# Gate logits turned by four transposes and summed on VectorE, and expert 0's first product taken in two halves of 256 tokens

## The chip, the cores and the metric

One Trainium2 chip, of which the kernel uses one core. The metric is device time in microseconds (us) of one execution, the median of the runs shown; less is better. A core has TensorE (PE in the rows, its weight loads PEld), VectorE (DVE), ScalarE (ACT), GpSimd (POOL), and SyncE (SP), which issues most of the transfers. Each engine takes its own instructions in the order in which the program gives them; engines wait for each other by semaphores.

## The reference

Three stages follow each other. A delta-rule attention (4 batches, 8 heads, 768 steps, head size 48) gives 3072 tokens of 384 features; a mixture of 8 experts with soft gates takes them; a last layer with x·cos(x) between two products ends it.

```python
for t in range(S):                                   # attention
    y[:, :, t] = einsum('bhd,bhde->bhe', q[:, :, t], state)
    v_old = einsum('bhde,bhd->bhe', state, k_n[:, :, t])
    state = state + beta_t * outer(k_n[:, :, t], v[:, :, t] - v_old)
...
logits = x @ w_gate                                  # 3072 x 8
P = exp(logits - logits.max())
for _ in range(8):                                   # balance rows and columns
    P /= P.sum(1, keepdims=True) + 1e-09
    P /= P.sum(0, keepdims=True) + 1e-09
    P *= N / E
for e in range(E):
    h = maximum(x @ w1[e], 0.0)
    out += P[:, e:e + 1] * (h @ w2[e])
...
h = x @ w_in
return (h * cos(h)) @ w_out
```

## The kernel before, in words

**Units and blocks.** The 768 steps are cut into 12 units of 64 steps; a unit of all heads and batches gives 256 tokens. Two units make a block of 512 tokens, and `xb[m]` holds block m twice, as a high part (written by ScalarE, L577) and a low part (what the high part left over, written by VectorE, L578). Products in the experts are taken as high·high, high·low and low·high, so 384 features in three slices of 128 give nine matmuls of 512 tokens.

**Expert 0 beside the attention.** While the attention runs, TensorE also does expert 0. `moe0_h` takes a *first product* (nine matmuls, `h_mms`, L138) for 128 hidden features of one block into the bank `hb`; ScalarE and VectorE apply the relu and split it in two parts (`relu_split`, L156 and L157). `moe0_y` takes the *second product* (nine matmuls, `yT_mms`, L150) into the three banks `yb[0]` to `yb[2]`. The half steps alternate: first product s+1, then second product s. All first products of this stage use the one bank `hb`, so each waits until VectorE's L157 has read the one before.

**The order** is written out by hand. `SEQ` has a string of letters for each unit, and `tick` runs them in turn on all engines. The string that matters begins `m W G E K r g m N m e O m m`, and belongs to unit 2, the first that works on block 0. `m` is a half step, `G` the gate logits of a block (`pe_gate`, six matmuls into `yb[0]`, copied to SBUF as `ltm`, 16 rows by 512 tokens: the first eight rows and the last eight have to be added), `E` turns queries, `K` multiplies the state with the keys (its difference D is VectorE's L513), `e` takes the query-key products (`pe_GQ`, L312, masked by VectorE's L367), `X` turns a unit's output into `xb` by six transposes (L572).

**The turning of the logits**, `g` (`pe_gate2`), multiplies four slices of 128 tokens of `ltm` by `two`, a 16x8 matrix of two stacked identities, which turns and adds at once (L597), into the first 32 columns of `yb[0]`. ScalarE copies them to `logits` (L600). It happens once for each block, six times: in the strings of units 2, 4, 6, 8, 10 and 11.

**The inverse.** Two units at a time, GpSimd solves small triangular systems in 60 steps, one after the other (L387 and L391), each depending on the last. `r` runs what is left of the steps and then gives VectorE a transpose of the result (`inv_dm`, L451), which waits for GpSimd.

**After the attention** eight rounds of row and column sums balance P: `sk_exp` and `sk_cols`, small matmuls (L622, L635) and VectorE steps, between products of expert 0. The exponential (L624) needs another ScalarE table than what went before, so a table load stands ahead of it. Most of the run, from about 450 us on, is the other experts and the last layer.

Of the kernel before, what the change touches and what calls it, by code (L numbers as in the profile page):

```python
# [8 lines left out]
F32 = mybir.dt.float32  # L9
F32R = mybir.dt.float32r  # L10
ACTF = mybir.ActivationFunctionType
ALU = mybir.AluOpType
# [10 lines left out]
I32 = mybir.dt.int32  # L23
BF16 = mybir.dt.bfloat16

SEQ = ("U0 a0 y1 o2 S0 x1 b0 P0 K1 o3 k1 v U1 X0 P1 S1 X1 x2",
# [12 lines left out]
def kernel(  # L39
# [13 lines left out]
    nc = tc.nc  # L53
    B, H, S, D = q.shape
    NT, DM = out.shape
    E, _, F = w1.shape
# [4 lines left out]
    KD = DM // 128  # L61
# [5 lines left out]
    const = ctx.enter_context(tc.tile_pool(name="const", bufs=1))  # L67
# [15 lines left out]
    hb, yb, pa = ps8[:, 0], [ps8[:, 1 + i] for i in range(KD)], [ps8[:, 4 + i] for i in range(4)]  # L83

    ident = const.tile([128, 128], F32, name="ident")
    wg_sb = const.tile([128, KD, E], F32, name="wg_sb")
    wg = const.tile([128, KD, 2, E], F32R, name="wg")
    logits = const.tile([128, NQ, E], F32, name="logits")
# [5 lines left out]
    Xsys = inv1[:, 0:1024].rearrange("p (t i) -> p t i", i=CB)  # L94
    Nst = inv2[:, 0:1024].rearrange("p (s t) -> p s t", t=CB)
    ltm = inv2[0:2 * E, 1024:1536]
    two = const.tile([2 * E, E], F32, name="two")
    ones = const.tile([128, 128], F32, name="ones")
    small = const.tile([128, 4, 32], F32, name="small")

# [27 lines left out]
        nc.scalar.activation(out=t[:, 0], in_=st, func=ACTF.Copy)  # L128
        eng.tensor_tensor(out=t[:, 1], in0=st, in1=t[:, 0].bitcast(F32), op=ALU.subtract)

    def h_mms(ps, n, f, x, c0, nn):

        w = w1_t[n]
        fs = slice((f % 2) * 128, (f % 2) * 128 + 128)
        i = 0
        for kk in range(KD):
            for a, b in ((0, 0), (0, 1), (1, 0)):
                nc.tensor.matmul(  # L138
                    out=ps[:, :nn], lhsT=w[:, a, kk, fs], rhs=x[:, b, kk, c0:c0 + nn],
                    start=(i == 0), stop=(i == 3 * KD - 1),  # L140
                )
                i += 1

    def yT_mms(banks, n, f, h, first, last):

# [43 lines left out]
    kr, qr, V, KT, QT, Pp, Go, D_t, U_t, Y_t, xb = {}, {}, {}, {}, {}, {}, {}, {}, {}, {}, {}  # L189
# [404 lines left out]

    def pe_gate2(m):
        for i in range(4):
            nc.tensor.matmul(  # L597
                out=yb[0][:, i * E:(i + 1) * E], lhsT=ltm[:, i * 128:(i + 1) * 128], rhs=two, start=True, stop=True,
            )
        nc.scalar.activation(  # L600
            out=logits[:, 4 * m:4 * m + 4, :], in_=yb[0][:, 0:4 * E].rearrange("p (i e) -> p i e", i=4), func=ACTF.Copy
        )


    sk = []
# [59 lines left out]
    def moe0_h(s):  # L665
        m, f = divmod(s, FT)

        if s >= NS0 - 4:
            bank, h = (pa[2], pa[1], pa[0], hb)[s % 4], htile()
        else:  # L670
            bank = pa[0] if scr and s % 2 else hb
            h = hp.tile([128, 2, 512], F32R, tag="h", name="h")
        h_mms(bank, f // 2, f, xb[m], 0, 512)
        relu_split(h, bank, 512)
        h0_t[s] = h

# [17 lines left out]
    with tc.manual_schedule():  # L694
# [36 lines left out]
        for r in range(4):  # L731
            m = m16[r * CB:(r + 1) * CB]
            nc.gpsimd.affine_select(
                out=m, in_=m, pattern=[[1, CB]], compare_op=ALU.is_gt, fill=0.0, base=0, channel_multiplier=-1
# [9 lines left out]
        for b in range(2):  # L744
            m = mask[b * C:(b + 1) * C]
            nc.gpsimd.affine_select(
                out=m, in_=m, pattern=[[1, C]], compare_op=ALU.is_gt, fill=0.0, base=0, channel_multiplier=-1
            )
        nc.gpsimd.memset(St[0], 0.0)
        nc.gpsimd.tensor_tensor(out=two, in0=ident[0:2 * E, 0:E], in1=ident[0:2 * E, E:2 * E], op=ALU.add)  # L750
        nc.gpsimd.memset(ones, 1.0)

        inv_q = []
# [167 lines left out]
        for s in range(NS0 - 1):  # L921
            t = 2 * ((s + 1) // FT) + 2
# [5 lines left out]
        def half():  # L928
            if mq and mq[0][0] <= done[0]:
                _, c, s = mq.pop(0)  # L930
                (moe0_h if c == "h" else moe0_y)(s)
# [9 lines left out]
        def tick(u, seq):  # L941
            early = u < 2
            for x, c in enumerate(seq.split()):
# [4 lines left out]
                    u, c = int(c[1]), c[0]  # L948
                if c == "m":
                    half()  # L950
                elif c == "K":
                    pe_KS(u)
                elif c == "k":
# [970 lines left out]
```

## Time and profile before

| | |
|---|---|
| median of 3 runs | 2100.38 us (2097.69 to 2106.63) |
| the profiled execution | 2102.24 us, of which 2100.5 us is the span from first to last instruction |
| busy TensorE | 2056.9 us, 98% of the span |
| busy VectorE, ScalarE, GpSimd | 1467.1, 859.2, 905.2 us |
| chain of work that ended last | TensorE 91%, DMA 3%, VectorE 2%, GpSimd 2% |
| mean granted TensorE clock | 0.988 of 2.4 GHz |

How to read it: the chain that ended last runs over TensorE nearly throughout, so a microsecond of TensorE work or of TensorE idleness is a microsecond of the run, unless something else sets the pace at that place. TensorE's idle time is 2100.5 - 2056.9 = 43.6 us. The slices of the page show where it lies: in the first 100 us TensorE is busy in seven to nine tenths, later in nine tenths or more of every slice.

### The profile page before, as it was taken

The page shows a single profiled execution, that of the slowest core. Times are in us where ns is not written, and L with a number is a line of the kernel's source. Part 1 is how long each engine was busy: PE and PEld are TensorE (multiplying, and loading weights), DVE is VectorE, ACT ScalarE, POOL GpSimd, SP SyncE. Part 2 cuts the span into 40 slices and gives each one's busy share as a digit, 9 for nine tenths or more (in the row PEclk, how much of TensorE's full clock was granted, in tenths as well). Part 3 has the DMA queues.
Part 4 walks back from the last instruction along what each step waited for, and adds up shares of the span by engine and source line. Part 5 has one row for each costly group of instructions (what it writes and reads, how often), then busy time and mean ns, then how long its engine had stood idle before and what let it go on. Part 6 is the DMA issues. An engine that isn't in the chain of part 4 may idle for free.

```text
span 2100.5 us, 39722 instructions
## 1 busy us (share of the span) xinstructions
PE 2056.9 (98%) x16147; PEld 1732.4 (82%) x16147; DVE 1467.1 (70%) x2247; ACT 859.2 (41%) x1436; POOL 905.2 (43%) x1013
## 2 busy tenths in 40 slices
PE   7899999999999999999999999999999999999999
PEld 6788787778888888888878888888888889999998
DVE  6665546677777777778767778778778666666665
ACT  3343333334444344343333333333333346666664
POOL 4676660136556565454344333333333343333232
PEclk6899999999999999999999999999999999999999
DMA  5442335765455445453684444435353551011000
GB/s 97 109 108 49 85 111 182 264 258 189 151 198 179 165 171 202 138 193 133 242 322 133 163 165 151 150 109 196 139 180 134 177 223 31 1 31 31 16 16 15
DMA packets 212470, 294.39 MB, mean 140 GB/s; under 512 B 86160, under 2 KB 159344, under 8 KB 212288
## 3 DMA queue, kind: packets, MB, share of 16 engines
q1 hardware_dynamic: 209456, 285.08, 40.7%
q0 software_dynamic: 1664, 6.49, 0.9%
q8 instruction: 126, 2.06, 0.4%
q10 hardware_dynamic: 1168, 0.30, 0.1%
q14 instruction: 56, 0.46, 0.1%
HBM read 188.95 MB, written 113.87 MB: 144 GB/s over the span
## 4 chain that ended last, share of the span: by engine, by line
PE 91%; DMA 3%; DVE 2%; POOL 2%; issue 1%; ACT 1%; SPq 0%; POOLq 0%; DVEq 0%; ACTq 0%
PE ps L150 36%; PE ps L1462 26%; PE ps L1752 9%; PE ps L1710 9%; PE ps L138 4%; PE ps L312 1%; PE ps L280 1%; POOL w1t L391 1%; POOL w1t L387 1%; DMA T<-xsc 1%; DMA tp<-in_moe_w_out_dram 1%; DMA wss<-w1t 1%; PE ps L497 1%; PE ps L474 1%; PE ps L462 1%
## 5 line engine op out<-in xcount | busy, mean ns | idle before, releaser
L150 PE MATMUL ps<-mh,w2t 128*128 128x512 f32 x3060 | 749.5, 390 | 1.2 <-DVE cth L1498 1.2
L150 PEld LDWEIGHTS ps<-mh,w2t 128*128 128x128 f32 x3060 | 573.4, 188 | 123.4 <-DVE cth L1498 5.0
L1462 PE MATMUL ps<-T,w1t 128*128 128x512 f32 x2520 | 627.6, 390 | 3.8 <-DVE ps L1470 2.1
L1499 POOL TENSOR_TENSOR accp<-accp,cth 128x512 f32<-128x512 f32 x246 | 320.1, 1330 | 568.3 <-DVE cth L1498 568.2
L1462 PEld LDWEIGHTS ps<-T,w1t 128*128 128x128 f32 x2520 | 472.1, 188 | 104.1 <-DVE ps L1470 3.4
L156 ACT ACTIVATE mh<-ps 128x512 fp32r<-128x512 f32 x340 | 203.4, 599 | 623.9 <-PE ps L1462 237.3
L157 DVE SCALAR_TENSOR_TENSOR mh<-ps,mh 128x512 fp32r<-128x512 f32 x340 | 228.8, 688 | 176.5 <-ACT mh L156 174.8
L1467 ACT ACTIVATE scr<-ps 128x512 f32<-128x512 f32 x224 | 134.4, 600 | 171.0 <-PE ps L1462 164.2
L1719 POOL TENSOR_SCALAR tp<-tp 128x512 f32<-128x512 f32 x92 | 91.1, 990 | 204.6 <-ACT tp L1718 204.6
L1498 DVE TENSOR_TENSOR cth<-ps,scr 128x512 f32<-128x512 f32 x246 | 154.3, 683 | 15.3 <-PE ps L150 14.2
L1733 DVE TENSOR_TENSOR tp<-tp,ps 128x512 f32<-128x512 f32 x96 | 66.1, 688 | 133.5 <-ACT tp L1732 133.5
L1470 DVE TENSOR_TENSOR ps<-scr,ps 128x512 f32<-128x512 f32 x168 | 116.5, 694 | 56.8 <-PE ps L1462 55.4
L138 PE MATMUL ps<-xb,w1t 128*128 128x512 f32 x432 | 114.0, 409 | 5.9 <-DVE h L157 4.5
L138 PEld LDWEIGHTS ps<-xb,w1t 128*128 128x128 f32 x432 | 79.4, 192 | 24.6 <-DVE h L157 4.6
L150 PE MATMUL ps<-h,w2t 128*128 128x512 f32 x396 | 98.5, 393 | 0.0
L1470 DVE TENSOR_TENSOR scr<-ps,scr 128x512 f32<-128x512 f32 x112 | 77.1, 688 | 29.6 <-PE ps L1462 28.7
L1303 DVE TENSOR_TENSOR w1t<-wraw,w1t 128x512 fp32r<-128x512 f32 (+2 forms) x81 | 82.4, 1029 | 9.9 <-ACT w1t L1300 9.5
L391 POOL TENSOR_TENSOR w1t<-w1t 128x30 f32<-128x30 f32 (+9 forms) x150 | 81.5, 543 | 11.8
L150 PEld LDWEIGHTS ps<-h,w2t 128*128 128x128 f32 x396 | 73.3, 188 | 15.3
L1710 PE MATMUL ps<-xx,cw 128*128 128x512 f32 x360 | 84.0, 390 | 0.0
L1718 ACT ACTIVATE tp<-ps 128x512 f32<-128x512 f32 x96 | 56.1, 585 | 63.4 <-PE ps L1710 63.4
L387 POOL TENSOR_TENSOR w1t<-Nsys,w1t 128x30 f32<-128x30 f32 (+9 forms) x150 | 77.0, 514 | 11.4
(286 smaller groups left out, 2769.9 us busy)
## 6 DMA issues: line engine op xcount, KB each, us to landing
wss<-w1t SPq DMA_DIRECT2D x56, 768.0 KB
w1t<-wss SPq DMA_DIRECT2D x56, 768.0 KB
w2t<-w2c SPq DMA_DIRECT2D x56, 384.0 KB
T<-tsc SPq DMA_DIRECT2D x22, 512.0 KB
scr<-pts SPq DMA_DIRECT2D x44, 256.0 KB
w2c<-in_moe_w_dram SPq DMA_DIRECT2D x28, 384.0 KB
wss<-w1t SPq DMA_DIRECT2D x28, 384.0 KB
w1t<-wss SPq DMA_DIRECT2D x28, 384.0 KB
```

Source lines behind the costliest of these rows:

```text
L138: nc.tensor.matmul(out=ps[:, :nn], lhsT=w[:, a, kk, fs], rhs=x[:, b, kk, c0:c0 + nn], start=(i == 0), stop=(i == 3 * KD - 1),)
L150: nc.tensor.matmul(out=banks[kd], lhsT=w[:, a, f % 2, kd * 128:(kd + 1) * 128], rhs=h[:, b, :], start=(first and b == 0 and a == 0), stop= ...
L156: nc.scalar.activation(out=h[:, 0, :nn], in_=ps[:, :nn], func=ACTF.Relu)
L157: nc.vector.scalar_tensor_tensor(out=h[:, 1, :nn], in0=ps[:, :nn], scalar=0.0, in1=h[:, 0, :nn].bitcast(F32), op0=ALU.max, op1=ALU.subtract,)
L391: eng.tensor_tensor(out=xsys[:, j + 1:, 0:j], in0=xsys[:, j + 1:, 0:j], in1=a, op=ALU.add)
L1462: nc.tensor.matmul(out=bank, lhsT=s_of(n, nm, a), rhs=T[:, b, :], start=start and q == 0, stop=q == 2, skip_group_check=True)
L1467: nc.scalar.activation(out=out, in_=in_, func=ACTF.Copy, scale=scale)
L1470: nc.vector.tensor_tensor(out=out, in0=a, in1=b, op=op)
L1498: nc.vector.tensor_tensor(out=c, in0=yb[kd], in1=pslot[t], op=ALU.mult)
L1499: nc.gpsimd.tensor_tensor(out=a[:, kd, :], in0=a[:, kd, :], in1=c, op=ALU.add)
L1710: nc.tensor.matmul(out=hb2(i), lhsT=net_w1(f, a, kk), rhs=x2[b](c, kk), start=(j == 0), stop=(j == 3 * KD - 1))
L1752: nc.tensor.matmul(out=ybk[t][:, :DM], lhsT=h[:, a, ts], rhs=net_w2(f, c), start=(f == 0 and j == 0), stop=(f == FT2 - 1 and j == 2),)
```

## The change

Three things are altered. The turning of the logits uses four transposes of 16 rows instead of four matmuls with `two`, which leaves 16 columns for each token; ScalarE copies the last eight of them to `logits`, and a new VectorE instruction adds the first eight from the bank. The matrix `two` and the GpSimd instruction that made it are gone. Expert 0's very first product (s = 0) is cut in two: a new letter `H` in the string of the first units takes tokens 0 to 255 behind unit 1's output transposes (`X1`), and the half step `m` of unit 2 then takes tokens 256 to 511, with the three matmuls that need the low part of `xb` last. Relu and split of that product stay one step for all 512 tokens.

```diff
-SEQ = ("U0 a0 y1 o2 S0 x1 b0 P0 K1 o3 k1 v U1 X0 P1 S1 X1 x2",
+SEQ = ("U0 a0 y1 o2 S0 x1 b0 P0 K1 o3 k1 v U1 X0 P1 S1 X1 H0 x2",
...
-    two = const.tile([2 * E, E], F32, name="two")
...
-    def h_mms(ps, n, f, x, c0, nn):
+    def h_mms(ps, n, f, x, c0, nn, late=False):
...
-        i = 0
-        for kk in range(KD):
-            for a, b in ((0, 0), (0, 1), (1, 0)):
-                nc.tensor.matmul(
-                    out=ps[:, :nn], lhsT=w[:, a, kk, fs], rhs=x[:, b, kk, c0:c0 + nn],
-                    start=(i == 0), stop=(i == 3 * KD - 1),
-                )
-                i += 1
+        o = [(kk, a, b) for kk in range(KD) for a, b in ((0, 0), (0, 1), (1, 0))]
+        if late:
+            o.sort(key=lambda t: t[2])
+        for i, (kk, a, b) in enumerate(o):
+            nc.tensor.matmul(
+                out=ps[:, :nn], lhsT=w[:, a, kk, fs], rhs=x[:, b, kk, c0:c0 + nn],
+                start=(i == 0), stop=(i == 3 * KD - 1),
+            )
...
         for i in range(4):
-            nc.tensor.matmul(
-                out=yb[0][:, i * E:(i + 1) * E], lhsT=ltm[:, i * 128:(i + 1) * 128], rhs=two, start=True, stop=True,
-            )
-        nc.scalar.activation(
-            out=logits[:, 4 * m:4 * m + 4, :], in_=yb[0][:, 0:4 * E].rearrange("p (i e) -> p i e", i=4), func=ACTF.Copy
-        )
+            nc.tensor.transpose(
+                yb[0][:, i * 2 * E:(i + 1) * 2 * E], ltm[:, i * 128:(i + 1) * 128], ident[0:2 * E, 0:2 * E]
+            )
+        lt, lg = yb[0][:, 0:8 * E].rearrange("p (i a e) -> p i a e", i=4, a=2), logits[:, 4 * m:4 * m + 4, :]
+        nc.scalar.activation(out=lg, in_=lt[:, :, 1], func=ACTF.Copy)
+        nc.vector.tensor_tensor(out=lg, in0=lt[:, :, 0], in1=lg, op=ALU.add)
...
-        h_mms(bank, f // 2, f, xb[m], 0, 512)
+        if s == 0:
+            h_mms(bank[:, 256:512], 0, 0, xb[0], 256, 256, True)
+        else:
+            h_mms(bank, f // 2, f, xb[m], 0, 512)
...
-        nc.gpsimd.tensor_tensor(out=two, in0=ident[0:2 * E, 0:E], in1=ident[0:2 * E, E:2 * E], op=ALU.add)
...
+                elif c == "H":
+                    h_mms(hb, 0, 0, xb[0], 0, 256)
```

TensorE in unit 2's string, from the state-key product (`KT`) over the turning of block 0's logits (`two` or `ident` against `w2t`, the tile in which `ltm` lies) and the next first and second product to the query-key products (`QT,KT`); the name in brackets is the engine whose semaphore the instruction waits for. Before:

```order
L497 MATMUL ps_154<-S_184,KT 64x48 x32
L597 MATMUL ps_154<-two,w2t 128x8 [waits Activation_49]
L597 MATMUL ps_154<-two,w2t 128x8 x3
L138 MATMUL ps_154<-xb,w1t 128x512 [waits DVE_49]
L138 MATMUL ps_154<-xb,w1t 128x512 x8
L150 MATMUL ps_154<-h,w2t 128x512 [waits Activation_49]
L150 MATMUL ps_154<-h,w2t 128x512 x8
L312 MATMUL ps_154<-QT,KT 64x64 [waits DVE_49]
L312 MATMUL ps_154<-QT,KT 64x64 x31
L138 MATMUL ps_154<-xb,w1t 128x512 [waits DVE_49]
```

The same place in the changed kernel:

```order
L496 MATMUL ps_154<-S_183,KT 64x48 x32
L596 MATMUL ps_154<-ident,w2t 128x16 [waits Activation_49]
L596 MATMUL ps_154<-ident,w2t 128x16 x3
L138 MATMUL ps_154<-xb,w1t 128x512 [waits DVE_49]
L138 MATMUL ps_154<-xb,w1t 128x512 x8
L149 MATMUL ps_154<-h,w2t 128x512 [waits DVE_49]
L149 MATMUL ps_154<-h,w2t 128x512 x8
L311 MATMUL ps_154<-QT,KT 64x64 x32
L138 MATMUL ps_154<-xb,w1t 128x512 [waits DVE_49]
```

No instruction of this piece has moved, but the second product waits for VectorE where it waited for ScalarE, and the query-key products behind it have lost their own wait for VectorE.

VectorE at the same place, from the relu of the first product s = 0 over two weight splits, D, and the inverse's transpose to the relu of s = 1. Before:

```order
L157 SCALAR_TENSOR_TENSOR h<-ps_154,h 128x512 [waits Activation_49]
L129 TENSOR_TENSOR w1t<-stg,w1t 128x768 [waits DMAHW7_49,Activation_49]
L129 TENSOR_TENSOR w2t<-stg,w2t 128x768 [waits DMAHW0_49,Activation_49]
L513 TENSOR_TENSOR D<-v,ps_154 128x2x8x48 [waits DVE_49,PE_49]
L451 STREAM_TRANSPOSE dm<-w1t 128x32x32 [waits Pool_49]
L157 SCALAR_TENSOR_TENSOR h<-ps_154,h 128x512 [waits Activation_49]
```

And in the changed kernel:

```order
L156 SCALAR_TENSOR_TENSOR h<-ps_154,h 128x512 [waits Activation_49]
L128 TENSOR_TENSOR w1t<-stg,w1t 128x768 [waits DMAHW7_49,Activation_49]
L128 TENSOR_TENSOR w2t<-stg,w2t 128x768 [waits DMAHW0_49,Activation_49]
L512 TENSOR_TENSOR D<-v,ps_154 128x2x8x48 [waits DVE_49,PE_49]
L450 STREAM_TRANSPOSE dm<-w1t 128x32x32 [waits Pool_49]
L601 TENSOR_TENSOR logits<-ps_154,logits 128x32 [waits Activation_49]
L156 SCALAR_TENSOR_TENSOR h<-ps_154,h 128x512 [waits Activation_49]
```

The new add stands behind the transpose that waits for GpSimd and ahead of the relu of s = 1.

ScalarE at the exponential that follows the last block's logits. Before:

```order
L600 ACTIVATE logits<-ps_154 128x32 [waits PE_49]
L156 ACTIVATE h<-ps_154 128x512 [waits DVE_49,PE_49]
L624 ACT_TABLE_LOAD [waits DVE_49]
L624 ACTIVATE P<-logits,small 128x192 [waits Activation_49]
L1300 ACTIVATE w1t<-wraw 128x512 [waits DMAHW0_49,Pool_49]
```

In the changed kernel:

```order
L600 ACTIVATE logits<-ps_154 128x32 [waits PE_49]
L155 ACTIVATE h<-ps_154 128x512 [waits DVE_49,PE_49]
L623 ACT_TABLE_LOAD
L623 ACTIVATE P<-logits,small 128x192 [waits DVE_49]
L1303 ACTIVATE w1t<-wraw 128x512 [waits DMAHW0_49,Pool_49]
```

The wait for VectorE has moved from the table load to the exponential behind it.

## Rows read from the trace of the kernel before

**Rows 1.** Stretches: length; each engine's busy us (instructions); clock, DMA share, GB/s.
```profile
82.00:95.00 13.00, 8.53 (x91) 6.75 (x90) 7.29 (x13) 2.81 (x5) 4.49 (x13) 0.87 0.64 155
150.00:450.00 300.00, 288.78 (x5401) 236.36 (x5389) 174.20 (x278) 102.29 (x167) 118.15 (x221) 0.99 0.46 143
700.00:2100.00 1400.00, 1392.58 (x6402) 1184.94 (x6400) 1011.46 (x1541) 598.54 (x1001) 544.85 (x473) 1.00 0.39 134
```

**Rows 2.** Timeline, TensorE: start, us, operation xcount [idle before <- what ended it].
```profile
70.88 0.88 PE L572 MATMUL ps<-ident,Y 128*128 128x128 f32 x6
72.66 0.50 PE L138 MATMUL ps<-xb,w1t 128*128 128x512 f32 x1 [0.90 <-ACT xb L577]
73.65 2.14 PE L138 MATMUL ps<-xb,w1t 128*128 128x512 f32 x8 [0.49 <-DVE xb L578]
...
79.05 1.05 PE L597 MATMUL ps<-two,w2t 16*128 16x8 f32 x8
80.03 2.34 PE L138 MATMUL ps<-xb,w1t 128*128 128x512 f32 x9
82.21 2.20 PE L150 MATMUL ps<-h,w2t 128*128 128x512 f32 x9
84.34 1.16 PE L312 MATMUL ps<-QT,KT 48*64 48x64 f32 x64
89.98 3.66 PE L138 MATMUL ps<-xb,w1t 128*128 128x512 f32 x9 [4.47 <-DVE h L157]
93.48 2.24 PE L150 MATMUL ps<-h,w2t 128*128 128x512 f32 x9
95.55 1.03 PE L280 MATMUL ps<-ident,kr 128*128 128x128 f32 x8
```

**Rows 3.** Timeline, VectorE, the same stretch.
```profile
72.64 0.96 DVE L578 TENSOR_TENSOR xb<-ps,xb 128x768 fp32r<-128x768 f32 x1 [0.69 <-ACT xb L577]
...
79.27 0.94 DVE L513 TENSOR_TENSOR D<-v,ps 128x768 f32<-128x768 f32 x1
87.47 1.91 DVE L451 STREAM_TRANSPOSE dm<-w1t 128x1024 f32<-128x1024 f32 x1 [7.25 <-POOL w1t L391]
89.28 0.65 DVE L157 SCALAR_TENSOR_TENSOR h<-ps,h 128x512 fp32r<-128x512 f32 x1
...
90.90 1.22 DVE L367 TENSOR_TENSOR Pp<-ps,mask 128x1024 f32<-128x1024 f32 x1
...
94.37 0.69 DVE L157 SCALAR_TENSOR_TENSOR h<-ps,h 128x512 fp32r<-128x512 f32 x1
```

**Rows 4.** Timeline, GpSimd, the last step of the first inverse.
```profile
87.18 0.25 POOL L391 TENSOR_TENSOR w1t<-w1t 128x30 f32<-128x30 f32 x1
```

**Rows 5.** Stretches around the restart at 89.98; the third figure from the end is the clock.
```profile
88.00:90.00 2.00, 0.02 (x1) 0.03 (x1) 2.00 (x3) 0.00 (x0) 0.00 (x0) 0.86 1.18 122
92.00:93.00 1.00, 1.00 (x4) 0.78 (x3) 0.86 (x6) 0.00 (x0) 0.00 (x0) 0.57 0.00 0
```

**Rows 6.** Timeline, VectorE, a two-input operation of 128x32 that reads PSUM.
```profile
42.56 0.19 DVE L788 TENSOR_TENSOR beta_sb<-beta_sb,ps 128x32 f32<-128x32 f32 x1 [0.55 <-PE ps L780]
```

**Rows 7.** Timeline, TensorE, a later turning (unit 6) and what follows it.
```profile
215.84 1.05 PE L597 MATMUL ps<-two,w2t 16*128 16x8 f32 x8
216.83 1.20 PE L474 MATMUL ps<-tx,W 32*32 32x32 f32 x64
...
220.13 2.20 PE L150 MATMUL ps<-h,w2t 128*128 128x512 f32 x9
```

**Rows 8.** Timeline, VectorE, beside it.
```profile
215.98 0.95 DVE L513 TENSOR_TENSOR D<-v,ps 128x768 f32<-128x768 f32 x1
218.11 0.95 DVE L234 TENSOR_REDUCE nrm<-sq 128x16 f32<-128x768 f32 x1 [1.17 <-ACT sq L231]
```

**Rows 9.** Timeline, ScalarE, the table load ahead of the exponential.
```profile
401.25 1.28 ACT L624 ACT_TABLE_LOAD   x1 [2.15 <-DVE small L623]
```

**Rows 10.** Timeline, TensorE, the first column sum behind the exponential.
```profile
405.69 0.39 PE L635 MATMUL ps<-small,ones 128*128 128x8 f32 x2 [0.43 <-DVE small L632]
```

## The prediction

> **What bounds the kernel now.** I read the busy time by stretch first. From 700 us on TensorE is busy for 1392.6 of 1400 us [rows 1], so what starts late there ends late: a delay or gain before that point goes through to the end nearly whole. Between 150 and 450 us it idles 11.2 us in all, and between 82 and 95 us it is busy for only 8.5 of 13 us, with the clock at 0.87 [rows 1]. The second view is TensorE's timeline. Its largest single wait, 4.47 us, ends at 89.98, where the first product s = 2 waits for VectorE's relu of s = 1 [rows 2]. The third is VectorE's timeline there: the relu runs at 89.28, not because its own input was late, but because it stands behind the transpose L451, and VectorE idled 7.25 us ahead of that, waiting for GpSimd [rows 3]. GpSimd's last step of the inverse ends at 87.43 [rows 4], and L451 starts 0.04 us later. So from 72 to 90 us the pace is set by the inverse on GpSimd, and TensorE's work up to there has slack; from 90 us on TensorE sets it again.
>
> **The halved first product.** Before, s = 0 started at 72.66 after waiting 0.90 us for the high part, and waited 0.49 us more for the low part of `xb` [rows 2]; VectorE writes that at 72.64 to 73.60 [rows 3]. In the changed kernel nine half-width matmuls run behind the transposes of 70.88, and nine more follow, of which three wait for the low part. A matmul of 256 tokens isn't in the trace; the neighbours are 128 columns (six transposes in 0.88 us, at most 0.15 us each) and 512 (nine in 80.03 to 82.21, 0.24 each) [rows 2]. At 0.15 the first nine fill 71.7 to 73.0, six end at 73.9 and three at 74.4, against 73.65 + 8 x 0.24 = 75.6 before: 1.2 us earlier. At 0.24 the eighteen take 4.3 us and end at 76.0, 0.4 us later. I take the gain, because half the columns should be nearer to the 128-column row, but neither end counts: what comes next is the stretch paced by the inverse, with 4.47 us of slack on TensorE. The same holds for the `two` product removed from GpSimd's set-up. Value at the end: 0. Were the cover gone, it would be worth -1.2 us.
>
> **The turning, removed and added.** The four matmuls with `two` appear as eight passes from 79.05 to 80.03, 0.98 us or 0.12 us a pass; in unit 6 it is 215.84 to 216.83 [rows 2, 7]. A transpose shows as one pass per instruction (six for six at 70.88 [rows 2]), so four transposes should take four passes: 0.49 us. Saved: 0.49 us per turning. Bounds: nothing, if the small transposes cost as much as what they replace, up to 0.6 us at the shortest spacing that the rows allow (eight transposes at 95.55 within 1.03 us, the last one's tail included [rows 2]). I take 0.49, since the row counts passes. Of the six turnings, the first lies in the covered stretch and gains nothing; the other five lie in stretches where TensorE runs without a gap before and behind (216.83 starts as 215.84's passes end [rows 7]): 5 x 0.49 = **-2.45 us**.
>
> The new add: 128x32 with one input from PSUM took 0.19 us [rows 6]. At the five later turnings it stands behind D. In unit 6 D ends at 216.93, VectorE then idles 1.17 us before 218.11 [rows 8], and the second product that overwrites `yb[0]` starts at 220.13 [rows 7], 3 us later. So there the add is hidden, and the new wait is met long before: 0. The cover would be gone if VectorE reached the add over 3 us after D.
>
> **The new wait at the first turning.** Here the order matters more than the cost. In unit 2's string `r` comes ahead of `g`, so the add stands behind L451, which can't start before GpSimd is done at 87.43. The second product s = 0, which writes `yb[0]`, now waits for VectorE, and this must be the add: the query-key products behind it lost a wait that covered D, so the wait ahead of them covers an instruction from D on, and the product itself needs nothing of D, of the transpose, or of the relu of s = 1. Before, that product and the query-key products ran at 82.21 and 84.34, ahead of the wait [rows 2]; now both are queued behind it on TensorE, and so is VectorE's masking L367 behind them.
>
> The add takes the place of the relu at 89.28 and ends at 89.47; TensorE restarts about 0.05 us later, as it did at 89.98 after the relu's 89.93 [rows 2, 3]: 89.52. Then: second product s = 0 at the low clock, 3.50 us (89.98 to 93.48, the same nine matmuls of 512 columns) to 93.02; query-key products 1.16 to 94.18; first product s = 2 at full clock 2.18 (80.03 to 82.21) to 96.36; second product s = 1, 2.07 (93.48 to 95.55) to 98.43. Before, this point was at 95.55 [rows 2]: **+2.9 us**. VectorE keeps up: L367 moves from 90.90 to about 94.3, and the relu of s = 2 with it from 94.37 to about 97.8, before TensorE needs it at 99.2. Nothing in the attention runs to an outside clock from there (the next inverse starts from products that move along), so the shift stays.
>
> The clock: at 89.98 the granted clock was at 1.2 GHz already. 88 to 90 has a mean of 0.86, so it fell at about 89.4, and 92 to 93 has 0.57, so 2.4 GHz came back at about 92.9 [rows 5]. The low stretch cost 3.50 - 2.07 = 1.4 us. I take the same cost again, as the idle stretch before is only longer (about 8 us instead of 4.47). If 2.4 GHz came with the restart the term would be +1.5; if all nine matmuls and the query-key products ran at half speed, (4.14 - 3.50) + 1.16 = 1.8 more, +4.7. The Trainium skill (TensorE: Matmul & The Clock Gate, part 1, "What's actually happening") holds that an idle engine is throttled and that activity releases it, at a moment that depends on where the first matmul falls and so differs between runs; that speaks against lengthening this wait, and by it the term may lie anywhere between those two ends. The trace shows one such release, 2.9 us after the restart.
>
> **The exponential.** The table load (1.28 us at 401.25) waited for VectorE [rows 9]; in the changed kernel it doesn't, only the exponential does, so it can run in the 2.15 us in which ScalarE idled ahead of it. The balancing then starts 1.28 us earlier, and TensorE's wait of 0.43 us at 405.69 [rows 10] goes: **-0.43 us**, and no more, as second products stand next. Bounds: 0 and -0.43.
>
> **Sum.** 0 + 2.9 - 2.45 - 0.43 = 0.0 us. The profiled execution took 2102.24 us (span 2100.5 and 1.7 around it), 0.09% above the median; so it stays at 2102.2, and the median at 2100.4.
>
> **Rivals.** *The hold at the first turning isn't there*, since the wait was for something earlier. Then only the add ahead of the relu costs, 0.15 us: 0.15 - 2.45 - 0.43 = -2.7, 2097.7. The lost wait of the query-key products speaks against it.
> *The transposes are no cheaper.* Price: the five gains of 0.49 go, 2.9 - 0.4 = +2.5, 2102.9. One pass per transpose in the rows is against it; a fixed cost of small matmuls for it.
> *Slower for good: the add holds the second product at all six turnings.* 6 x 2.9 - 2.9 = +14.5, 2114.9. It decides where VectorE reaches the add over 3 us after D; with VectorE idle there [rows 8] it should not.
> *The low clock lasts longer or shorter* at the restart: +1.8 or -1.4, 2102.2 or 2099.0.
> *The change does what it seems to, the halved product's 1.2 us reaching the end*: 2099.2. It needs the inverse to end earlier, and nothing in the diff touches its steps.
>
> **How the numbers follow.** Forecast, no change at 2100.4: 0.74. No hold 0.07, transposes no cheaper 0.08, hold at all six 0.03, clock 0.05, halved product 0.01; 0.02 for what I don't see, half on each side. A measurement of this kernel can tell about 0.5%, 10.5 us, from no change; all cases but the six holds lie within: same 0.95, slower 0.04, faster 0.01. The range takes in no hold (2097.7) and dear transposes (2102.9), widened by the runs' own spread (2.7 us below the median, 6.3 above): 2096 to 2106.
>
> **What would show it.** Right: the second product s = 0 starts near 89.5 behind the add, and the key transposes near 98.4 instead of 95.55; later turnings last near 0.5 us and the second product behind each follows without a gap; no wait at the first column sum. Wrong: a second product before 88 us (no hold), TensorE waits for the add in later units, turnings of 1 us, or GpSimd's inverse ending away from 87.4.

## The result and the profile after

The changed kernel takes 2130.84 us (median of 4 runs, 2125.86 to 2135.64) against 2100.80 us (4 runs) for the kernel before, run beside it: a ratio of 1.0131, 95% interval 1.0112 to 1.0149. It is 1.3% slower where no change was predicted. The profiled execution took 2130.78 us, its span is 2129.0 us, 28.5 us more than before.

The page of the changed kernel, its first parts and the chain that ended last:

```profile
span 2129.0 us, 39697 instructions
PE 2082.4 (98%) x16132; PEld 1730.8 (81%) x16132; DVE 1465.5 (69%) x2253; ACT 859.2 (40%) x1436; POOL 904.8 (42%) x1012
...
PE 89%; POOL 3%; DMA 2%; DVE 2%; issue 1%; SPq 1%; ACT 0%; POOLq 0%; DVEq 0%; ACTq 0%
```

TensorE is busy 25.5 us longer (2082.4 against 2056.9) while the other engines have the same work. Only 3.0 of the 28.5 us are idle time of TensorE; for the rest it works more slowly. To see where, I matched the matmuls of both traces one by one and took the difference of their start times, each counted from the first instruction of its own trace. It is +3.3 us at the key transposes of 95.55, falls to +0.8 at 352 us and +0.1 at 404, and is -0.6 at 407 and +0.1 at 464, where the other experts are under way. Then it grows evenly: +9.6 at 980, +15.5 at 1254, +24.7 at 1695, +28.3 at 2094. From the exponential to 464 us the balance is within 0.6 us of the predicted 0.0. All the loss comes behind it, in matmuls that the diff doesn't touch.

The same 200 us in that stretch, before and then after (columns as in [rows 1]):

```profile
1300.00:1500.00 200.00, 200.00 (x884) 165.57 (x883) 157.74 (x245) 65.51 (x108) 67.74 (x48) 1.00 0.44 150
```

```profile
1300.00:1500.00 200.00, 200.00 (x866) 162.22 (x865) 154.39 (x242) 62.79 (x103) 66.61 (x48) 1.00 0.44 149
```

TensorE is busy without a gap and at full clock in both, yet does 866 matmuls instead of 884: 200 / 884 = 226 ns each before, 231 ns after. The 1392.6 busy us of 1400 that the prediction started from [rows 1] hide this: a matmul that takes longer is just as busy. TensorE's timeline in that stretch, before and then after:

```profile
1400.30 2.20 PE L150 MATMUL ps<-mh,w2t 128*128 128x512 f32 x9
1402.34 2.20 PE L1462 MATMUL ps<-T,w1t 128*128 128x512 f32 x9
1404.38 2.20 PE L150 MATMUL ps<-mh,w2t 128*128 128x512 f32 x9
```

```profile
1400.15 2.24 PE L149 MATMUL ps<-mh,w2t 128*128 128x512 f32 x9
1402.23 1.56 PE L1465 MATMUL ps<-T,w1t 128*128 128x512 f32 x6
1403.63 2.23 PE L149 MATMUL ps<-mh,w2t 128*128 128x512 f32 x9
```

Before, nine take 2.04 us whichever product they belong to, 226.8 ns each. After, the first products (L1465: weights in `w1t`, tokens in `T`) take 1.40 us for six, 233 ns each, and the second products (`mh`, `w2t`) 2.08 us for nine, 231 ns each. Over all records the spacings within a product are 226.8 ns for both before, and 233.5 and 230.0 ns after. That is 2520 x 6.7 ns = 16.9 us, plus 2726 x 3.2 ns = 8.7 us (second-product matmuls that follow one of their own), minus 1.2 us of waits that became shorter: 24.4 us, against the 24.6 by which the shift grows from 464 to 1695 us.

The grouped rows by line say the same, and add the last layer, where the rest of the loss (3.6 us) arises. Before, then after (busy us, mean ns of one, idle before):

```profile
L1462 PE MATMUL ps<-T,w1t 128*128 128x512 f32 x2520 | 627.6, 390 | 3.8 <-DVE ps L1470 2.1 <-ACT ct L1467 1.3 <-ACT scr L1467 0.2
...
L1710 PE MATMUL ps<-xx,cw 128*128 128x512 f32 x360 | 84.0, 390 | 0.0
...
L1710 PE MATMUL ps<-xx,w2t 128*128 128x512 f32 x120 | 29.2, 390 | 0.0
```

```profile
L1465 PE MATMUL ps<-T,w1t 128*128 128x512 f32 x2520 | 644.4, 396 | 2.9 <-ACT ct L1470 1.3 <-DVE ps L1473 1.2 <-ACT scr L1470 0.2
...
L1713 PE MATMUL ps<-xx,cw 128*128 128x512 f32 x360 | 85.9, 395 | 0.0
...
L1713 PE MATMUL ps<-xx,w2t 128*128 128x512 f32 x120 | 29.1, 389 | 0.0
```

The slower groups here pair a tile of the left side of SBUF (`w1t`, `xx`), which the program lays out from the low addresses up, with one of the right side (`T`, `cw`); `xx` with `w2t`, both on the left, kept its pace. The second products (`mh` with `w2t`, both on the left) are an exception: they slowed too. That points at where the tiles lie. `two` was a tile of 16x8 floats, 32 bytes in every partition. It stood ahead of the large tiles of the left side, and with it gone all of them begin 32 bytes lower in the program's placement of tiles (byte addresses within a partition): `w1t` at 19872 where it was at 19904, `w2t` at 50592 (50624), `mh` at 134560 (134592), `xx` at 132512 (132544). `T` and `cw`, laid out from the other end, stay at 167360. Before, all of these begin at the same place modulo 512 bytes (448).

### The profile page after: what moved, and what is told of

Its sections match the earlier page's. It is cut to its first block, busy times and chain, and to the rows that moved or that the text cites. A ratio compares the mean times of both kernels' runs of the same rounds, so it can differ in the third digit from the quotient of the medians.

```text
span 2129.0 us, 39697 instructions
## 1 busy us (share of the span) xinstructions
PE 2082.4 (98%) x16132; PEld 1730.8 (81%) x16132; DVE 1465.5 (69%) x2253; ACT 859.2 (40%) x1436; POOL 904.8 (42%) x1012
## 4 chain that ended last, share of the span: by engine, by line
PE 89%; POOL 3%; DMA 2%; DVE 2%; issue 1%; SPq 1%; ACT 0%; POOLq 0%; DVEq 0%; ACTq 0%
PE ps L149 36%; PE ps L1465 27%; PE ps L1755 9%; PE ps L1713 9%; PE ps L138 4%; POOL w1t L390 2%; POOL w1t L386 2%; PE ps L311 1%; DMA T<-xsc 1%; DMA tp<-in_moe_w_out_dram 1%; PE ps L279 1%; DMA T<-tsc 0%; SPq L208 0%; PE ps L473 0%; PE ps L461 0%
## 5 line engine op out<-in xcount | busy, mean ns | idle before, releaser
L149 PE MATMUL ps<-mh,w2t 128*128 128x512 f32 x3060 | 758.8, 392 | 0.8 <-DVE cth L1501 0.8
L1465 PE MATMUL ps<-T,w1t 128*128 128x512 f32 x2520 | 644.4, 396 | 2.9 <-ACT ct L1470 1.3
L1465 PEld LDWEIGHTS ps<-T,w1t 128*128 128x128 f32 x2520 | 472.0, 188 | 116.2 <-DVE ps L1473 3.2
L138 PE MATMUL ps<-xb,w1t 128*128 128x512 f32 (+1 forms) x441 | 113.4, 402 | 0.0
L1275 POOL TENSOR_TENSOR w2t<-w2t 128x768 fp32r<-128x768 f32 x28 | 56.0, 1999 | 58.1 <-ACT w2t L1271 58.1
```

The source lines that it names most:

```text
L138: nc.tensor.matmul(out=ps[:, :nn], lhsT=w[:, a, kk, fs], rhs=x[:, b, kk, c0:c0 + nn], start=(i == 0), stop=(i == 3 * KD - 1),)
L149: nc.tensor.matmul(out=banks[kd], lhsT=w[:, a, f % 2, kd * 128:(kd + 1) * 128], rhs=h[:, b, :], start=(first and b == 0 and a == 0), stop= ...
L1465: nc.tensor.matmul(out=bank, lhsT=s_of(n, nm, a), rhs=T[:, b, :], start=start and q == 0, stop=q == 2, skip_group_check=True)
```

## The experiments

Two theories stood first. By *placement*, the matmuls are slower because the left side has moved against the right. By *the work*, the new turning, its waits or the halved product set off something that lasts (other overlaps of transfers and engines in the experts).

### The 32 bytes given back

One line is added to the changed kernel, where the line of `two` stood:

```diff
+    const.tile([2 * E, E], F32, name="pad")
```

> The changed kernel with an unused tile of 32 bytes per partition where the removed 16x8 matrix lay, so that every later tile is back at its old place in SBUF; all instructions are those of the changed kernel. Theory P (place): the changed kernel loses its 28 us because 32 bytes fewer in the first pool shift every weight and activation tile of that side, and the experts' matmuls then follow each other at 233.5 (product with w1) and 230.0 ns (product with w2) instead of 226.8. By P this run is at 2100 to 2103 us and both spacings are 226.8 again. Theory W (work): the loss comes from the changed work itself (the hold, the later start, transfers that now collide): 2125 to 2136 us, spacings as in the changed kernel.

Measured: 2104.15 us, ratio to before 0.999 (95% interval 0.9978 to 1.0002, as in all brackets behind a ratio). The window:

```profile
1300.00:1500.00 200.00, 200.00 (x884) 165.56 (x883) 157.39 (x246) 65.42 (x108) 69.23 (x50) 1.00 0.44 150
```

884 again, and spacings of 226.8 and 226.9 ns. A tile that nothing reads takes the whole loss back. It also measures the work of the change by itself: nothing that can be told from zero in time.

### The kernel before with 32 bytes less

`two` is put into a free corner of another tile, `small`, so only its own tile disappears; the turning stays the old one.

```diff
-    two = const.tile([2 * E, E], F32, name="two")
...
+    two = small[0:2 * E, 3, 8:8 + E]
```

> The kernel before with its 16x8 matrix put into an unused corner of another tile, so that its 32 bytes go and every later tile shifts by 32 bytes, with no instruction changed in kind or order. P: 2126 to 2133 us, spacings 233.5 and 230.0 ns in the experts, while the first 450 us stay as before. W: 2098 to 2105 us, both at 226.8 ns.

Measured: 2126.53 us, ratio 1.0108 (1.0079 to 1.0137), 233.6 and 230.0 ns for first and second products, and 866 matmuls in the window:

```profile
1300.00:1500.00 200.00, 200.00 (x866) 162.22 (x865) 153.89 (x240) 64.13 (x105) 68.25 (x48) 1.00 0.44 153
```

The loss is there without any of the change's work. Matched with the kernel before as above, this kernel loses 29.5 us between 412 us and the end, and the changed kernel 28.9 us. Its profiled execution is only 22.0 us longer than that of the kernel before because it was 7.6 us ahead by 412 us: the inverse ended 3.2 us sooner, and TensorE's clock didn't fall around 318 us. Nothing in the edit bears on either, so I count both as differences from one execution to the next.

### Both sides moved, and the right side alone

A pad lies at the end of SBUF behind `T`. Eight floats more of it move `T` down by the same 32 bytes as the left side of the changed kernel:

```diff
-        tpool.tile([128, 136], F32, name="Tpad")
+        tpool.tile([128, 144], F32, name="Tpad")
```

> The changed kernel with the tiles T (the moving operand of the products with w1, on the other side of SBUF) moved down by 32 bytes too, through a larger pad behind them. P with distance (what counts is the place of the weights against that of the moving operand): the product with w1 is back at 226.8 ns, the product with w2 (whose two operands had kept their distance) is not explained by it and stays at 230: about 2130.8 - 2520 x 6.7 ns = 2114 us. P with place alone (each tile by itself has to lie on a multiple of 64 bytes): 233.5 ns stays or grows, 2130 us or more. W: 2126 to 2136 us with no change in the spacings.

Measured: 2107.19 us, ratio 1.0012 (1.0000 to 1.0024), 884 matmuls. I had expected the second product to stay at 230 ns and some 2114 us; that was wrong, it recovered too. The last layer did not, since `cw` hadn't moved:

```profile
L1713 PE MATMUL ps<-xx,cw 128*128 128x512 f32 x360 | 85.9, 395 | 0.0
...
L1755 PE MATMUL ps<-cw,nh 128*128 128x384 f32 x432 | 79.2, 338 | 0.0
```

These are the changed kernel's values. In the last layer alone this kernel loses 3.6 us on the kernel before (+3.5 to +7.1), as the changed kernel does there.

The other way round, the kernel before with eight floats less, so that `T` alone moves up by 32 bytes:

```diff
-        tpool.tile([128, 136], F32, name="Tpad")
+        tpool.tile([128, 128], F32, name="Tpad")
```

> The kernel before with only the tiles T moved up by 32 bytes, everything else where it was. P with distance: product with w1 at 233.5 ns, product with w2 at 226.8: about 2100.8 + 2520 x 6.7 ns = 2118 us. P with the weights' place alone: 2098 to 2105 us, since the weights have not moved. P with the moving operand's place alone: about 2118 us here, and then e3 slow as well. W: 2098 to 2105 us.

Measured: 2125.92 us, ratio 1.0094 (1.0073 to 1.0115):

```profile
1300.00:1500.00 200.00, 200.00 (x866) 162.22 (x865) 154.42 (x242) 62.80 (x103) 66.73 (x48) 1.00 0.44 149
```

866 again, with `xx` against `cw` at its old 390 ns. From 412 us on it loses 25.3 us, the changed kernel's 28.9 less the 3.6 of the last layer. Neither side's own place matters; their distance does. I had expected the second products to stay at 226.8 ns and 2118 us: they slow down here although neither `mh` nor `w2t` has moved. In the records the first five of the eight spacings within a run of nine average 229 to 235 ns, and the last three 227 to 228. That looks like something that the first products set off and that lasts into the next run; no run shows it.

### Which distances are harmless

> The kernel before, with the tiles T (the moving operand of the last layer's products from xb's split and of the experts' products) 64 bytes nearer to the end of SBUF and everything else where it was, so that the distance between weights and T changes by 64 bytes instead of 32. If what costs time is that the distance stops being a multiple of 64 bytes, this is free: 884 matmuls in 200 us, spacing 226.8 ns, time as before (2100 to 2105). If any departure from the old places costs (a particular pair of addresses that was lucky), it is as slow as with 32 bytes: 866 in 200 us, about 2126.

Measured: one time of 2122.56 us, 869 matmuls in the window. My rule (multiples of 64 bytes are free) fell. The pattern differs:

```profile
L150 PE MATMUL ps<-mh,w2t 128*128 128x512 f32 x3060 | 765.2, 394 | 0.9 <-DVE cth L1498 0.8
L1462 PE MATMUL ps<-T,w1t 128*128 128x512 f32 x2520 | 633.8, 392 | 3.0 <-DVE ps L1470 1.4 <-ACT ct L1467 1.3 <-ACT scr L1467 0.3
```

Now the second product, whose tiles haven't moved, loses more (394 ns where it had 390) than the first (392 for 390). So three larger steps, in the same line: 104, 72 and 8 floats instead of 136.

> The kernel before with T alone 128 bytes nearer to the end of SBUF. In the kernel before, the weights, T, and the experts' hidden tiles all begin at the same place modulo 512 bytes, so every distance among them is a multiple of 512; 32 and 64 bytes off were both slow, 64 in another pattern. If the period is 128 bytes, this is as fast as before (226.8 ns, 884 matmuls in 200 us, 2100 to 2106); if it is 512, this is slow (at least 2115).

> T alone moved by 256 bytes. Period 128 or 256: as before, 226.8 ns and 2100 to 2106. Period 512: slow, at least 2115, or by less than with 128 bytes if the cost falls with the distance.

> T alone moved by 512 bytes, the size of one weight slice's row and the step between all slices of a tile. If what counts is the distance modulo 512 or a part of it, this is as before: 226.8 ns, 884 matmuls in 200 us, 2100 to 2106. If any move of T away from its old place costs, whatever the distance, this is slow too, and the distance is not the cause.

Measured, one time each: 2123.14, 2104.60 and 2105.35 us, beside 2105.45 for the kernel before. The windows for 128 and then for 256 bytes:

```profile
1300.00:1500.00 200.00, 200.00 (x870) 162.84 (x869) 154.45 (x243) 65.28 (x107) 66.52 (x48) 1.00 0.45 153
```

```profile
1300.00:1500.00 200.00, 200.00 (x884) 165.57 (x883) 158.09 (x246) 65.31 (x107) 67.73 (x48) 1.00 0.44 150
```

Distances off by 32, 64 and 128 bytes cost 18 to 22 us; 256 and 512 cost nothing that one time each can tell, and their spacings are the old 226.8 and 226.9 ns. Of the distances tried, the multiples of 256 bytes are the free ones. The kernel before had all its large tiles at one place modulo 512, and the 32 bytes of `two` were part of what held them there.

### The change's own parts

The halves alone, on the kernel before, with `two` and the old turning kept:

```diff
-    ... U1 X0 P1 S1 X1 x2
+    ... U1 X0 P1 S1 X1 H0 x2
...
+        if s == 0:
+            h_mms(bank[:, 256:512], 0, 0, xb[0], 256, 256, True)
```

> The kernel before with the halved product alone, the matrix two and the old turning kept, so that no place in SBUF changes. If the loss comes from the 32 bytes alone, this is as before: ratio 1.000 within 0.001, 884 matmuls in 200 us. If the halves themselves cost or gain, it shows here: 1.2 us of gain would be a ratio of 0.9994, about the limit of what can be told.

Measured: 2106.22 us, ratio 1.0009 (0.9992 to 1.0025), 226.8 ns: by time, no difference that can be told. From the output transposes to the first gate product it takes 3.24 us (71.21 to 74.45) where it took 4.74 before (70.88 to 75.62). That 1.5 us is an earlier arrival at the wait for the inverse, which the halves don't touch. TensorE's clock falls in that wait, here as in the kernel before:

```profile
83.20 1.16 PE L312 MATMUL ps<-QT,KT 48*64 48x64 f32 x64
87.96 4.21 PE L139 MATMUL ps<-xb,w1t 128*128 128x512 f32 x9 [3.60 <-DVE h L157]
91.96 3.12 PE L150 MATMUL ps<-h,w2t 128*128 128x512 f32 x9
94.92 1.03 PE L280 MATMUL ps<-ident,kr 128*128 128x128 f32 x8
```

In this profile TensorE waited 3.60 us, less than the 4.47 of the kernel before [rows 2], as the inverse ended at 85.41. Behind the wait eighteen matmuls take 6.96 us (87.96 to 94.92), where at full clock they take 4.46 (86.96 to 91.42 in the last kernel below): the clock granted from 88 to 90 us is 0.50, the 1.2 GHz level.

The new turning alone: the changed kernel with the pad tile and without the halves:

```diff
-    ... S1 X1 H0 x2
+    ... S1 X1 x2
...
-        if s == 0:
-            h_mms(bank[:, 256:512], 0, 0, xb[0], 256, 256, True)
-        else:
-            h_mms(bank, f // 2, f, xb[m], 0, 512)
+        h_mms(bank, f // 2, f, xb[m], 0, 512)
```

> The changed kernel with the 32 bytes given back and without the halved product: the four transposes and the add alone. If the halves are worth nothing, as the prediction had it (covered by the inverse), the time is that of the changed kernel with the 32 bytes, 2104, and a ratio of 0.999 to before. If their 1.2 us reach the end, or if they cost something, the ratio differs from 0.999 by 0.0006 or more. At the first gate logits I expect 75.6 us in both.

Measured: 2102.91 us, ratio 0.9993 (0.9978 to 1.0008), the same as with halves by time. Its gate logits came at 80.57, not at 75.6, as its TensorE ran at a low clock there (mean 0.67 from 72 to 80), so that part of the expectation says nothing of the halves.

The hold removed: the changed kernel with the pad tile, and with `r` and `g` of unit 2 swapped, so that VectorE has the add ahead of the transpose that waits for GpSimd:

```diff
-       "m W G E K r g m N m e O m m M t O m w R ...
+       "m W G E K g r m N m e O m m M t O m w R ...
```

> The changed kernel with the 32 bytes given back by an unused tile, and with the letters r and g of unit 2 swapped, so that VectorE's new add stands ahead of the transpose that waits for GpSimd. If the hold at the first turning is what the add costs, the second product s = 0 starts at 81 to 82 us, TensorE's wait moves to the first product s = 2 and shrinks to 2 to 5 us, the key transposes start at 91.5 to 95.6 instead of 98.8 (changed kernel) and 100.1 (with the 32 bytes alone), and the time is 3 to 5 us below that kernel: 2099 to 2101, a ratio to before of about 0.998. If the hold costs nothing because the stretch is paced by something later, the time stays at 2104.

Measured: 2102.02 us, ratio 0.9992 (0.9977 to 1.0006); 2.1 us below the kernel with the pad alone where I had expected 3 to 5, and the runs' spread doesn't separate that from nothing. The hold is gone, but TensorE's wait of 4.00 us is followed by a low clock in both products, and the key transposes start at 97.34, later than expected:

```profile
85.14 1.16 PE L312 MATMUL ps<-QT,KT 48*64 48x64 f32 x64
90.30 4.21 PE L139 MATMUL ps<-xb,w1t 128*128 128x512 f32 x9 [4.00 <-DVE h L157]
94.30 3.20 PE L150 MATMUL ps<-h,w2t 128*128 128x512 f32 x9
97.34 1.04 PE L280 MATMUL ps<-ident,kr 128*128 128x128 f32 x8
```

Since the inverse ends at another time in each profile (84.3 to 87.9 us), I compare what lies between the end of GpSimd's last step and the key transposes. Each row is one profiled execution; "held" means that the add stands behind the transpose that waits for GpSimd:

| turning, order, halves | inverse ends | key transposes | between | TensorE's wait | clock behind it |
|---|---|---|---|---|---|
| old (32 bytes less) | 84.27 | 91.32 | 7.05 | 1.70 | full |
| old (`T` 32 up) | 86.43 | 93.46 | 7.03 | 2.05 | full |
| old (`T` 64 up) | 85.34 | 92.40 | 7.06 | 1.48 | full |
| old (`T` 128, 256, 512 up) | 85.78, 85.83, 87.56 | 93.18, 94.26, 94.78 | 7.41, 8.43, 7.21 | none | full |
| old (kernel before) | 87.43 | 95.55 | 8.12 | 4.47 | low, 2.9 us |
| old, halves | 85.41 | 94.92 | 9.51 | 3.60 | low |
| new, held, no halves | 86.42 | 96.13 | 9.71 | 1.44 | full |
| new, held, halves (pad) | 87.90 | 100.12 | 12.22 | 8.51 | low |
| new, held, halves (changed kernel) | 86.50 | 98.82 | 12.32 | 6.82 | low |
| new, held, halves (both sides moved) | 86.56 | 98.56 | 12.00 | 10.41 | low |
| new, swapped, halves | 87.75 | 97.34 | 9.59 | 4.00 | low |

Two losses add up here: 9.71 - 7.05 = 2.7 us for the hold, at full clock, and 8.12 - 7.05 = 1.1 to 9.51 - 7.05 = 2.5 us where the clock falls in the wait. That the halves bring on the second is argued: they take TensorE to the wait 1.5 us sooner, but the kernel before waited 4.47 us without them, and how long the wait is changes with the end of the inverse. In the three profiles without a wait TensorE itself was late, after a low clock that lasted there until 72.9 to 81.4 us. The table asks for a kernel without hold and halves: the pad, the new turning, the swap.

> The changed kernel with the 32 bytes given back, the letters r and g of unit 2 swapped and without the halved product: four transposes and the add, with the add ahead of the wait for GpSimd. From GpSimd's last inverse step to the key transposes took 7.0 to 7.1 us in kernels with the old turning, no halves and the clock at full speed, 9.71 with the new turning ahead of which the add is held (no halves), and 9.59 with the swap but with halves, where TensorE idled 4.00 us and its clock fell. If the hold and the long idle time are two separate losses, both are gone here: 7.0 to 7.1 us, no low clock after 86 us, and a time of 2099 to 2102, a ratio to before of 0.9975 to 0.999. If the swap only moves the loss elsewhere, 9 us or more and about 2103 as without it.

Measured: 2097.98 us (12 runs) beside 2103.22 for the kernel before, ratio 0.9973 (0.9960 to 0.9986), a little below the expected range and the only kernel here whose interval lies wholly below that of no change.

```profile
83.70 1.16 PE L312 MATMUL ps<-QT,KT 48*64 48x64 f32 x64
86.96 2.37 PE L139 MATMUL ps<-xb,w1t 128*128 128x512 f32 x9 [2.09 <-DVE h L157]
89.16 2.21 PE L150 MATMUL ps<-h,w2t 128*128 128x512 f32 x9
91.42 1.09 PE L280 MATMUL ps<-ident,kr 128*128 128x128 f32 x8
```

The inverse ended at 84.40, so 7.02 us lie between, at full clock. Of the 5.2 us gained, the later turnings and the exponential explain about 3.8 (below), which the interval (2.9 to 8.4 us) covers alone; that the rest is in part the clock that the kernel before loses in this stage is argued. The intervals of the two kernels that take away only the hold (0.9992) or only the halves (0.9993) overlap with this one, so the two losses are shown in the profiles and not one by one in time.

## Why the prediction was wrong, point by point

**What bounds the kernel: right as far as it went.** TensorE still sets the end. The step that failed stands in this part: "what starts late there ends late: a delay or gain before that point goes through to the end nearly whole". It takes for granted that the matmuls behind that point keep their pace. They did not: 28 us came after 464 us.

**The removed matrix: the term that was missing.** The prediction costed `two` by its instruction ("The same holds for the `two` product removed from GpSimd's set-up. Value at the end: 0.") and never as a tile. Its 32 bytes moved the left side of SBUF, and that is worth 22 to 27 us by time (2126.53 - 2104.19 with the tile alone removed, 2130.84 - 2104.15 with it given back) and 29 us in the matched traces. So this is the term that failed: put at 0, it measured more than all the others together. No rival had it. What the profile before could have told: nothing in its rows; the placement of the tiles could have raised the question, as all of them begin at the same place modulo 512 and one piece of what holds them there was taken out, but no row of before prices it.

**The halved product: right by time.** Its first step gained a little more than estimated (1.5 us from the output transposes to the gate logits, against 1.2), since a matmul of 256 tokens takes about 0.144 us. In the changed kernel 18 of them run back to back, with the gate logits behind them at 75.61:

```profile
73.01 2.76 PE L138 MATMUL ps<-xb,w1t 128*128 128x256 f32 x18
```

That the gain is covered by the inverse held as well (ratio 1.0009 for the halves alone). That covered idle time can cost something, because the clock falls in it, was left out for this part; where it falls, the table has 1.1 to 2.5 us, and whether the halves make it fall isn't shown.

**The new wait at the first turning: the mechanism right, the size near in part by luck.** TensorE, VectorE and the granted clock in the changed kernel:

```profile
79.40 2.33 PE L138 MATMUL ps<-xb,w1t 128*128 128x512 f32 x9
88.55 4.21 PE L149 MATMUL ps<-h,w2t 128*128 128x512 f32 x9 [6.82 <-DVE logits L601]
92.68 1.99 PE L311 MATMUL ps<-QT,KT 48*64 48x64 f32 x64
94.60 2.34 PE L138 MATMUL ps<-xb,w1t 128*128 128x512 f32 x9
96.78 2.21 PE L149 MATMUL ps<-h,w2t 128*128 128x512 f32 x9
98.82 1.03 PE L279 MATMUL ps<-ident,kr 128*128 128x128 f32 x8
```

```profile
86.53 1.91 DVE L450 STREAM_TRANSPOSE dm<-w1t 128x1024 f32<-128x1024 f32 x1 [5.98 <-POOL w1t L390]
88.34 0.15 DVE L601 TENSOR_TENSOR logits<-ps,logits 128x32 f32<-128x32 f32 x1
88.41 0.68 DVE L156 SCALAR_TENSOR_TENSOR h<-ps,h 128x512 fp32r<-128x512 f32 x1
```

```profile
85.00:90.00 5.00, 1.45 (x4) 1.17 (x5) 3.43 (x5) 0.00 (x0) 1.19 (x5) 0.50 0.91 195
90.00:94.00 4.00, 4.00 (x55) 2.96 (x57) 0.16 (x1) 0.22 (x1) 0.00 (x0) 0.50 0.00 0
94.00:95.00 1.00, 1.00 (x30) 0.84 (x23) 0.26 (x1) 0.00 (x0) 0.00 (x0) 0.73 0.00 0
```

The second product waits for the add, the add stands behind the transpose, and the transpose behind GpSimd [rows 3, 4]. The restart came 1.0 us sooner than worked out (88.55 for 89.52), as the inverse ended 0.93 us sooner. The clock stayed at half through all nine matmuls and the query-key products, as in the rival *the low clock lasts longer*: 88.55 to 94.60 is 6.05 us where 4.66 was forecast. Together +3.3 us for +2.9. Two misses partly cancel here: counted from the end of the inverse, which the prediction had fixed at 87.43, the hold and its clock cost 12.32 - 8.12 = 4.2 us, not 2.9. The rule cited there (the Trainium skill, TensorE: Matmul & The Clock Gate, "What's actually happening") let the term lie anywhere between +1.5 and +4.7; the measured one lies between them, and the low clock ended 6 us behind the restart this time, 2.9 us before [rows 5].

**The turning: mis-sized by a good quarter.** Unit 6 in the changed kernel, to set beside [rows 7]:

```profile
218.32 0.42 PE L596 MATMUL ps<-ident,w2t 16*128 16x16 f32 x4
218.67 1.20 PE L473 MATMUL ps<-tx,W 32*32 32x32 f32 x64
```

Four transposes take 0.35 us (218.32 to 218.67), 0.09 each, where the four matmuls took 0.98: 0.63 us saved, beyond even the bound of 0.6; five times that is 3.15 us for 2.45, and the shift falls by 3.1 us between 100 and 404 us. The rival that they are no cheaper is out. The add in unit 6 (0.18 us at 219.33, behind D) holds nothing up in the rows, as forecast. A transpose is one pass and its pass is also shorter: one pass per instruction was counted, the pass itself taken at the old length.

**The exponential: the mechanism right, the size small.** The table load starts at 399.24, behind the relu before it and without a wait for VectorE; the exponential starts at 401.32, where it started at 402.55 in the kernel before; and the column sum (L634) has no wait ahead of it:

```profile
399.24 1.28 ACT L623 ACT_TABLE_LOAD   x1
401.32 0.46 ACT L623 ACTIVATE P<-logits,small 128x192 f32<-128x192 f32 x1 [0.79 <-DVE small L622]
```

```profile
405.23 0.28 PE L634 MATMUL ps<-small,ones 128*128 128x8 f32 x2
```

The shift falls from +0.1 to -0.6 there, 0.7 us where [rows 10] had let the prediction expect 0.43 and no more: the start of the column sum moves by 0.6 us, and its two matmuls end 0.1 us sooner behind it. So the sum of the work is 3.3 - 3.15 - 0.7 = -0.6 us, as read at 407 us, near the forecast's 0.0, and the kernel with the 32 bytes given back shows it in time (ratio 0.999, an interval of 4.6 us below to 0.4 above). The forecast answered the question of the work and missed that of the place.

## What to carry to other kernels

A tile that is removed or resized moves all that is allocated behind it; before costing such an edit, compare where the operands of the matmuls that fill the run begin, and keep the distance between tiles that TensorE uses together as it was, if need be by a pad. When busy time rises with the same count of instructions and a full clock, count matmuls per stretch before looking for waits. Idle time of TensorE that something else covers isn't free if the clock falls in it: here the matmuls behind it then took 1.1 to 2.5 us longer, at the upper end nearly as much as the hold.

## What the runs showed of the hardware that I had not expected

In these kernels the spacing of matmuls of 512 columns with a weight load each changes with the distance in a partition between `T`, the first products' moving operand, and the tiles of the left side, their weights among them: 226.8 ns when the distance is unchanged or differs by 256 or 512 bytes; 233.6 ns (first product) and 230.0 ns (second) at 32 bytes, 229.1 and 231.5 at 64, 232.4 and 229.2 at 128. In the last layer `xx` with `cw` does the same at 32 bytes (395 ns of one for 390), and `xx` with `w2t` doesn't. Smaller steps than 32 bytes and other multiples weren't tried.

Why is open. In the traces the weight load of the next matmul starts some 3 ns after each matmul's start and lasts 188 ns in both kernels, so the two reads of SBUF run side by side; a collision between them would fit the first products, and that it is a collision is argued, not shown. Nor did a run separate these two reads from what other engines and transfers do with the same tiles. The Trainium skill (SBUF — State Buffer, "Who interferes with whom") names only the port pair that VectorE and GpSimd share as a place of contention. By that rule `T`'s place could not matter to TensorE; the runs differ from it by 18 to 22 us for a move of `T` alone by 32 to 128 bytes, and the measurement decides.

That the second products slow down with `T` moved, though their own two tiles lie as before, was not expected either; no run here separates its cause.
